# New orders for three engines' lists in a two-layer linear-attention and MLP kernel, and two weight loads issued later

## The chip, the cores and the metric

The kernel runs on one core of a Trainium2 chip. Five engines work side by side in it: TensorE (PE in the profile; its weight loads are PEld), VectorE (DVE), ScalarE (ACT), GpSimd (POOL), and SyncE (SP), which only issues DMAs here. The metric is the device time of one execution in microseconds (us); of several runs the median is given.

## The reference

The input x has 2048 tokens of 512 values. Two layers run one after the other with the same weights. Each is a linear attention and an MLP, both behind a layer norm and both added to x:

```python
phi = lambda t: jnp.where(t > 0, t + 1, jnp.exp(t)) + 1e-6
pq, pk = phi(q), phi(k)                       # 32 heads of 16
kv  = jnp.einsum("bhsd,bhse->bhde", pk, v)
z   = jnp.einsum("bhsd->bhd", pk)
num = jnp.einsum("bhqd,bhde->bhqe", pq, kv)
den = jnp.einsum("bhqd,bhd->bhq", pq, z)[..., None] + 1e-6
x = x + (num / den) @ wo                      # attention, on layernorm(x)
x = x + gelu(layernorm(x) @ w1 + b1) @ w2 + b2    # w1: 512 x 1792
```

## The kernel before, in words

**Tiles.** Tokens lie in 16 tiles of 128 (index st) and 4 chunks of 512 (index c). V is never made: with y the normalised input, the kernel forms G = y'·phi(K) (512 x 512) and from it K'V. The names carry the layer as the code counts it: 0 is layer one, 1 is layer two.

**Names and lines.** Each operation has a name: its kind, the layer, and the tile or chunk and part.

- Norm of a tile: stats (L742), aggr (L744), veps (L755, L747), pow (L757, POOL), nmr (L774), norm (ACT L777 or DVE L782). Its transpose is a DMA issued by SP (TA before the attention, TB before the MLP, L792), or PE products (PT, L805) with a copy tc (L815).
- K and Q: products L860, L878, L891. Each is followed by phi: exp (ACT L830), relu (ACT L841), min (DVE L843), and the sum phi (L847, on DVE or POOL). In the other form it is min (L834) and phi (L836) on DVE, without relu.
- G: L961 in layer one, where it stays in four PSUM banks until the copies cpg0_0 to cpg0_3 (DVE L977). In layer two it is made by chunks (L993), gathered by ga (L1000, L1003) and gt (L1006).
- z: za (L914) sums phi(K) tiles, zhi (L920) and zlo (L923) split the sum in two, ZH (L930) and Z (L942) are products, zsh and zs (L934, L951) and zb (L1022) and dz (L1027) prepare it, ZR (L1030) and cpz (L974) make a row of it.
- K'V: KV (L1016, four short products for each of four row blocks of G), kvm (DVE mask, L1035), M (times wo, L1039), cpm (L974 on ACT, L977 on DVE).
- Denominators: D (L1085), ln (L1087) and rec (L1089) on ACT, pr (L1093) for some chunks. Others go by token: pz (L1061), red (L1064), den (L1067), rec (L1069), pr (L1073), and a transpose TP by SP (L1077).
- WO: L1109, and the sum RA (L1114). MLP: W1 products L1141, gelu (ACT L1147), W2 products L1180, RB (L1186, L1190), the output DMA OD (L1192).
- Late weight loads from POOL's queue (L682): w1_1, wv, wo, w1_0, w2_0, w2_1.

**What sets the order.** Nothing is decided on the chip. `CONF["ORDER"]` holds, for each engine, the list of its operations by name. A planner (`Scheduler.run`) plays the five lists against each other with assumed durations. It gives each tile a PSUM bank or a buffer when its first user is placed, the one that is free first, so that an order also settles which earlier users a tile has to wait for. The buffers that count here: 4 of exp (eb), 4 of relu (rb), 8 of phi(K) (pkb), 2 of ln (lr), 12 of chunks (t4). `assign_waits` turns every dependency on another engine into a semaphore wait, and `play` issues the list:

```python
for o in order[eng]:
    if o.table is not None and o.table != table:
        table = o.table
        e.preload_act_table_set(sets[table])
    for s, v in o.waits:
        e.wait_ge(s.h, v)
    ins = o.fn(e)
```

An engine works its list strictly in order: what waits holds all that stands behind it.

Of the kernel before, what the change touches and what calls it, by code (L numbers as in the profile page):

```python
# [282 lines left out]
def assign_waits(graph, order, sems, dma_sems):  # L283
# [10 lines left out]
    while len(done) < total:  # L294
        moved = False
        for e in ENGINES:
# [117 lines left out]
        "dve":  # L414
# [962 lines left out]
```

## Time and profile before

| what | us |
|---|---|
| median of 3 runs | 326.45 (326.38 to 326.69) |
| the profiled execution | 326.46 |
| its span, first to last instruction | 324.7 |
| outside the span | 1.76 |
| PE busy | 320.7 (1729 matmuls) |
| DVE, ACT, POOL busy | 218.6, 195.2, 134.9 |
| DMA moved | 20.39 MB, 63 GB/s in the mean |

How to read it: "busy" of PE includes the pipeline's own latency, and a row of the timeline runs from the start of its first instruction to the end of its last. So a stall of PE is read from the starts: four 512-column products that follow each other without a wait start 0.216 us apart, the next group 0.864 us behind the first. A number in square brackets is the idle time of the engine ahead of the row, with what ended it.

### The profile page before, as it was taken

What the parts mean: (1) busy time and instruction counts of PE and PEld (TensorE: products, weight loads), DVE (VectorE), ACT (ScalarE), POOL (GpSimd) and SP (SyncE); (2) the same over time, 40 slices, a digit from 0 to 9 for tenths busy, and PEclk for the clock granted to TensorE, in tenths of its full rate; (3) what the DMA queues carried; (4) which work ended last, traced back from release to release, by engine and by line L of the source; (5) the groups of instructions that cost most, each with busy time, mean ns of one, the idle gap of its engine ahead of it and who ended that gap; (6) DMA issues with size and microseconds to landing.
All of it is one profiled execution on the core that took longest, in us unless ns stands there. A gap on an engine that the chain in (4) does not pass through costs nothing.

```text
span 324.7 us, 4792 instructions
## 1 busy us (share of the span) xinstructions
PE 320.7 (99%) x1729; PEld 158.4 (49%) x1729; DVE 218.6 (67%) x506; ACT 195.2 (60%) x336; POOL 134.9 (42%) x224
## 2 busy tenths in 40 slices
PE   8999999999999999999999999999999999999996
PEld 4444544675444444444444444458644444444443
DVE  5997779999985760213759999999999564000232
ACT  6999698773136129488974567869832543576000
POOL 4673276628803259000266735683541754000000
PEclk9999999999999999999999999999999999999999
DMA  7524558112320205310003200022133123000004
GB/s 241 179 43 89 145 166 296 42 38 49 77 52 5 46 16 91 74 32 2 0 0 68 48 16 2 17 50 50 33 67 81 33 51 81 16 0 2 32 27 153
DMA packets 47028, 20.39 MB, mean 63 GB/s; under 512 B 42076, under 2 KB 45532, under 8 KB 47004
## 3 DMA queue, kind: packets, MB, share of 16 engines
q1 hardware_dynamic: 45532, 15.06, 20.2%
q0 software_dynamic: 1056, 4.72, 4.5%
q10 hardware_dynamic: 416, 0.30, 0.3%
q8 instruction: 14, 0.23, 0.3%
q14 instruction: 10, 0.08, 0.1%
HBM read 8.00 MB, written 2.10 MB: 31 GB/s over the span
## 4 chain that ended last, share of the span: by engine, by line
PE 90%; DVE 6%; ACT 2%; DMA 1%; POOL 0%; issue 0%
PE ps L1141 30%; PE ps L1180 28%; PE ps L1109 9%; PE ps L860 7%; PE ps L878 5%; PE ps L993 3%; PE ps L961 3%; PE ps L891 2%; PE ps L1167 1%; DMA t<-in_A_x_dram 1%; DVE eb L843 1%; DVE gtb L977 1%; DVE gacc L1003 1%; DVE yb L782 1%; PE ps L942 1%; PE ps L805 1%
## 5 line engine op out<-in xcount | busy, mean ns | idle before, releaser
L1147 ACT ACTIVATE gT<-ps,b1c 128x512 bf16<-128x512 f32 (+1 forms) x140 | 77.0, 600 | 63.3 <-PE ps L1141 62.6
L1141 PE MATMUL ps<-t,w 128*128 128x512 bf16 (+1 forms) x560 | 101.4, 336 | 0.0
L1180 PE MATMUL ps<-w,gT 128*128 128x512 bf16 x434 | 98.2, 379 | 0.0
L1141 PEld LDWEIGHTS ps<-t,w 128*128 128x128 bf16 x560 | 54.6, 98 | 43.9 <-ACT t L815 0.3
L1180 PEld LDWEIGHTS ps<-w,gT 128*128 128x128 bf16 x434 | 42.5, 98 | 50.0
L757 POOL TENSOR_TENSOR rstd<-veps,neghalf 128x1 f32<-128x1 f32 x64 | 38.7, 616 | 5.3 <-DVE veps L755 3.1
L830 ACT ACTIVATE eb<-ps 128x512 bf16<-128x512 f32 x56 | 32.6, 600 | 12.4 <-PE ps L860 5.5
L1190 DVE TENSOR_TENSOR pkb<-ps,xsb 128x512 bf16<-128x512 f32 x15 | 10.1, 684 | 40.7 <-PE ps L1180 40.7
L742 DVE BATCH_NORM_STATS2 stats<-xsb 128x6 f32<-128x512 f32 x48 | 32.2, 678 | 0.4
L860 PE MATMUL ps<-wqkv,t 128*128 128x512 bf16 x128 | 31.4, 379 | 0.1
L1109 PE MATMUL ps<-gtb,t 128*128 128x512 bf16 x128 | 30.9, 379 | 0.0
L841 ACT ACTIVATE rb<-ps 128x512 bf16<-128x512 f32 x38 | 22.1, 602 | 8.0 <-PE ps L860 6.6
L747 POOL TENSOR_SCALAR veps<-mv 128x1 f32<-128x1 f32 x32 | 8.7, 271 | 43.8 <-DVE mv L744 40.9
L755 POOL TENSOR_SCALAR veps<-mv 128x1 f32<-128x1 f32 x28 | 7.3, 267 | 45.5 <-DVE mv L744 44.0
L777 ACT ACTIVATE yb<-xsb,nmr,rstd 128x512 bf16<-128x512 f32 x21 | 16.9, 809 | 11.7 <-POOL nmr L774 11.7
L782 DVE TENSOR_SCALAR yb<-xsb,mv,rstd 128x512 bf16<-128x512 f32 x27 | 15.7, 590 | 11.9 <-POOL rstd L757 11.7
L1186 DVE TENSOR_TENSOR xsb<-ps,xsb 128x512 f32<-128x512 f32 x16 | 10.9, 682 | 16.5 <-PE ps L1180 16.5
L843 DVE TENSOR_SCALAR eb<-eb 128x512 bf16<-128x512 bf16 x46 | 14.9, 333 | 7.8 <-ACT eb L830 7.6
L878 PE MATMUL ps<-wqkv,t 128*128 128x512 bf16 x80 | 20.1, 379 | 0.0
L860 PEld LDWEIGHTS ps<-wqkv,t 128*128 128x128 bf16 x128 | 12.2, 98 | 15.0 <-ACT t L815 0.5
L1109 PEld LDWEIGHTS ps<-gtb,t 128*128 128x128 bf16 x128 | 12.3, 97 | 14.3 <-ACT gtb L974 0.5
L1126 POOL TENSOR_TENSOR xsb<-xsb,b2b 128x512 f32<-128x512 f32 x14 | 17.3, 1235 | 1.0 <-DVE yb L782 0.7
(103 smaller groups left out, 395.7 us busy)
## 6 DMA issues: line engine op xcount, KB each, us to landing
w<-in_B_w_dram POOLq DMA_DIRECT2D x4, 896.0 KB, 7.2
out_dram<-pkb SPq DMA_DIRECT2D x15, 128.0 KB, 2.0
t<-in_A_x_dram SPq DMA_DIRECT2D x3, 512.0 KB, 6.9
t<-yb SPq DMA_TRANSPOSE x56, 2.5
wqkv<-in_A_wqkv_dram SPq DMA_DIRECT2D x1, 512.0 KB, 5.3
wqkv<-in_A_wqkv_dram POOLq DMA_DIRECT2D x1, 512.0 KB, 4.4
wo<-in_A_wo_dram POOLq DMA_DIRECT2D x1, 512.0 KB, 5.5
t<-t SPq DMA_TRANSPOSE x20, 2.4
```

Source lines behind the costliest of these rows:

```text
L742: G.op("dve", lambda e: e.bn_stats(stats[:, s.slot, :], src()), 602, reads=src_keys, writes=[k + "s"], tiles=[s, *src_tiles], prio=prio, n ...
L757: G.op("pool", lambda e: e.tensor_tensor(rstd[:, s.slot:s.slot + 1], veps[:, s.slot:s.slot + 1], neghalf[:], op=ALU.pow), 530, reads=[k + ...
L782: G.op("dve", lambda e: e.tensor_scalar(yb[:, y.slot, :], src(), stats[:, s.slot, 2:3] if by_act else mv[:, s.slot, 0:1], rstd[:, s.slot:s ...
L830: G.op("act", lambda e: e.activation(eb[:, et.slot, :], bank(bt), ACT.Exp, scale=factor()), 569 if by else 483, reads=[src_key, *more], wr ...
L841: G.op("act", lambda e: e.activation(rb[:, rt.slot, :], bank(bt), ACT.Relu, scale=factor()), 569 if by else 478, reads=[src_key, *more], w ...
L843: G.op("dve", lambda e: e.tensor_scalar(eb[:, et.slot, :], eb[:, et.slot, :], 1.0, 1e-6, op0=ALU.min, op1=ALU.add), 202, reads=[f"e{tag}"] ...
L860: ins = e.matmul(bank(b), lhsT=yTa(yT)[:, dt, k * P:(k + 1) * P], rhs=wqkv[:, dt, D:2 * D], start=(dt == 0), stop=(dt == DT - 1))
L878: ins = e.matmul(bank(b), lhsT=yTa(yT)[:, dt, k * P:(k + 1) * P], rhs=wqkv[:, dt, 0:D], start=(dt == 0), stop=(dt == DT - 1))
L1109: ins = e.matmul(bank(wb), lhsT=yTa(pq)[:, kt, k * P:(k + 1) * P], rhs=gtb[:, kt, :], start=(kt == 0), stop=(kt == DT - 1))
L1141: ins = e.matmul(bank(b, n), lhsT=w1[:, dt, ft * P:(ft + 1) * P], rhs=yTa(yT)[:, dt, k0 * P:k1 * P], start=(dt == 0), stop=(dt == DT - 1))
L1147: G.op("act", lambda e, ft=ft, b=b, k0=k0, k1=k1, n=n: e.activation(gT[:, g.slot, ft * 512 + k0 * P:ft * 512 + k1 * P], bank(b, n), ACT.Ge ...
L1180: ins = e.matmul(bank(b), lhsT=gT[:, g.slot, ft * 512 + k * P:ft * 512 + (k + 1) * P], rhs=w2[:, ft, :], start=(ft == 0), stop=(ft == FT - 1))
```

## The change

The lists of ACT, DVE, POOL and SP are put in another order in two places. PE's list stays the same, and so does every operation, its engine and its form. The diff, cut to the lines that move something:

```diff
         "act":
...
-            "reluq0_1_1 rec0_0_3 cpz0 ln0_0_2 rec0_0_2 ln0_1_0 expq0_2_0 rec0_1_0 ln0_1_1 b1c rec0_1_1 cpm0_1 cpm0_0 "
+            "reluq0_1_1 rec0_0_3 cpz0 ln0_0_2 rec0_0_2 ln0_1_0 expq0_2_0 rec0_1_0 ln0_1_1 rec0_1_1 b1c cpm0_1 cpm0_0 "
...
-            "reluq1_0_0 expq1_0_0 expq1_1_1 expk1_9 reluk1_8 expk1_8 reluk1_9 normA1_12 reluk1_11 expk1_11 expk1_10 "
-            "reluk1_10 reluq1_1_2 expk1_13 expk1_15 reluk1_13 reluk1_15 expq1_1_2 expk1_12 expk1_14 expq1_0_2 "
-            "expq1_0_1 reluq1_0_3 expq1_0_3 reluq1_0_1 reluq1_0_2 expq1_1_3 cpz1 ln1_0_0 rec1_0_0 reluq1_1_3 "
...
+            "reluq1_0_0 expq1_0_0 expq1_1_1 expk1_9 reluk1_8 expk1_8 reluk1_9 normA1_12 reluk1_11 expk1_11 reluq1_1_2 "
+            "expk1_10 expq1_1_2 reluk1_10 reluk1_13 reluk1_15 expk1_13 expk1_15 expk1_12 expq1_0_1 expk1_14 expq1_0_2 "
+            "expq1_0_3 reluq1_0_2 expq1_1_3 reluq1_0_1 reluq1_0_3 cpz1 ln1_0_0 rec1_0_0 reluq1_1_3 reluq1_3_1 ln1_0_1 "
...
         "dve":
...
-            "phiq0_0_1 dz0 minq0_1_0 minq0_1_2 phiq0_1_0 pr0_0_0 minq0_1_1 pr0_0_1 pr0_0_3 cpg0_0 cpg0_1 cpg0_2 "
+            "phiq0_0_1 dz0 minq0_1_0 minq0_1_2 phiq0_1_0 pr0_0_0 pr0_0_1 pr0_0_3 minq0_1_1 cpg0_0 cpg0_1 cpg0_2 "
...
-            "ga1_0_1 mink1_8 minq1_1_1 normA1_13 phik1_9 ga1_1_1 phiq1_1_1 phik1_8 normA1_15 mink1_11 RB0_14 "
-            "statsA1_14 minq1_0_0 aggrA1_14 mink1_10 phik1_11 phik1_10 normA1_14 ga1_1_3 mink1_15 phiq1_0_0 zhi1 "
-            "minq1_1_2 mink1_13 phiq1_1_2 mink1_12 zlo1 ga1_1_2 phik1_13 ga1_1_0 mink1_14 phik1_12 minq1_0_2 phik1_14 "
-            "minq1_0_1 zsh1 ga1_2_1 zs1_3 minq1_0_3 dz1 zb1 minq1_1_3 phiq1_0_2 phiq1_0_3 phiq1_0_1 gt1_1 ga1_2_2 "
...
+            "ga1_0_1 mink1_8 minq1_1_1 normA1_13 phik1_9 ga1_1_1 phiq1_1_1 phik1_8 normA1_15 RB0_14 statsA1_14 "
+            "aggrA1_14 minq1_0_0 mink1_11 phik1_11 minq1_1_2 mink1_10 normA1_14 phik1_10 phiq1_0_0 ga1_1_3 phiq1_1_2 "
+            "ga1_1_0 mink1_15 zhi1 mink1_12 zlo1 ga1_1_2 mink1_13 phik1_13 phik1_12 mink1_14 phik1_14 ga1_2_1 zsh1 "
+            "minq1_0_3 minq1_0_1 zs1_3 minq1_0_2 dz1 zb1 phiq1_0_3 phiq1_0_1 minq1_1_3 phiq1_0_2 gt1_1 ga1_2_2 "
...
-            "RA1_0 rec1_1_2 RA1_1 statsB1_0 rec1_1_3 statsB1_1 aggrB1_1 pr1_1_3 aggrB1_0 RA1_2 statsB1_2 phiq1_3_0 "
-            "aggrB1_2 RA1_5 normB1_0 RA1_3 statsB1_3 aggrB1_3 normB1_2 minq1_3_2 RA1_7 normB1_3 phiq1_3_2 RA1_6 "
...
+            "rec1_1_2 RA1_1 statsB1_0 rec1_1_3 aggrB1_0 statsB1_1 aggrB1_1 RA1_2 pr1_1_3 minq1_3_0 statsB1_2 aggrB1_2 "
+            "normB1_0 phiq1_3_0 RA1_5 RA1_3 statsB1_3 aggrB1_3 normB1_2 minq1_3_2 RA1_7 normB1_3 phiq1_3_2 RA1_6 "
...
         "pool":
...
-            "nmrA0_7 nmrA0_6 vepsA0_11 powA0_11 nmrA0_9 phik0_6 w1_1 phiq0_1_2 wv wo w2_1 w1_0 phiq0_1_1 pr0_0_2 "
-            "pr0_1_0 pr0_1_1 w2_0 pr0_1_2 pr0_1_3 vepsB0_1 powB0_1 vepsB0_0 powB0_0 b20_0 vepsB0_2 powB0_2 vepsB0_3 "
+            "nmrA0_7 nmrA0_6 vepsA0_11 powA0_11 nmrA0_9 phik0_6 w1_1 phiq0_1_2 wv wo w1_0 phiq0_1_1 pr0_0_2 pr0_1_0 "
+            "pr0_1_1 w2_0 w2_1 pr0_1_2 pr0_1_3 vepsB0_1 powB0_1 vepsB0_0 powB0_0 b20_0 vepsB0_2 powB0_2 vepsB0_3 "
...
-            "pr1_0_1 pr1_0_2 pz1_1_3 pr1_0_3 pr1_1_0 phiq1_3_1 pr1_1_2 vepsB1_1 powB1_1 nmrB1_1 vepsB1_0 powB1_0 "
+            "pr1_0_1 pr1_0_2 pz1_1_3 pr1_0_3 phiq1_3_1 pr1_1_0 pr1_1_2 vepsB1_0 vepsB1_1 powB1_1 nmrB1_1 powB1_0 "
...
         "sp":
...
-            "TA1_7 TA1_9 TA1_10 TA1_8 TA1_11 TA1_13 TA1_12 TA1_15 TA1_14 TP1_1_1 TP1_1_0 TP1_1_3 TP1_1_2 TB1_2 TB1_3 "
+            "TA1_7 TA1_9 TA1_10 TA1_8 TA1_11 TA1_13 TA1_12 TA1_15 TA1_14 TP1_1_1 TP1_1_0 TP1_1_2 TP1_1_3 TB1_2 TB1_3 "
```

The cut lines hold the rest of layer two's K'V stage, where the lists are reordered in the same way, and gelu names that only move to another line of the text. Since buffers go to whoever is placed first, some tiles in the two places also take another bank or buffer and so wait for other users; outside the two places the waits are the same, but for the numbers of some t4 buffers.

28 rows, old and new, of the table ORDER are left out of this document.

## The prediction

> **What bounds the kernel.** I read the page's busy times and clock first, then the timeline of PE alone for gaps between starts, then the timelines of DVE and POOL around each gap.
>
> ```profile
> PE 320.7 (99%) x1729; PEld 158.4 (49%) x1729; DVE 218.6 (67%) x506; ACT 195.2 (60%) x336; POOL 134.9 (42%) x224
> ```
>
> PE is busy throughout, and the row PEclk of the page is a 9, the highest digit, in all 40 slices. So time can only be won where PE's starts stand further apart than its pitch: 0.216 us for a 512-column product, so 0.864 for four, and 0.23 for the four short ones of a KV. Past the first 8 us I find two such places (and 0.10 us near 17.5). Layer one's K'V stage:
>
> ```profile
> 48.89 0.38 PE L1085 MATMUL ps<-t,zb 128*128 128x512 bf16 x1
> 49.20 0.40 PE L1016 MATMUL ps<-gtb,wqkv 128*128 128x128 bf16 x4
> 49.44 0.38 PE L1085 MATMUL ps<-t,zb 128*128 128x512 bf16 x1
> 49.80 0.40 PE L1016 MATMUL ps<-gtb,wqkv 128*128 128x128 bf16 x4
> 50.40 0.40 PE L1016 MATMUL ps<-gtb,wqkv 128*128 128x128 bf16 x4 [0.20 <-DVE gtb L977]
> 50.63 1.03 PE L878 MATMUL ps<-wqkv,t 128*128 128x512 bf16 x4
> 51.61 1.04 PE L1039 MATMUL ps<-wo,kvb 128*128 128x512 bf16 x4
> ```
>
> The excess is 49.20-48.89-0.216 = 0.10 ahead of KV0_1, 0.15 ahead of KV0_2, 0.37 ahead of KV0_3, and 51.61-50.63-0.864 = 0.11 ahead of M0_1: **0.73 us**. Layer two, the last phi(K) tiles:
>
> ```profile
> 190.37 1.03 PE L860 MATMUL ps<-wqkv,t 128*128 128x512 bf16 x4
> 191.53 0.18 PE L930 MATMUL ps<-onesm,dz 128*128 128x1 bf16 x1
> ...
> 193.47 1.03 PE L878 MATMUL ps<-wqkv,t 128*128 128x512 bf16 x4
> 194.66 0.55 PE L942 MATMUL ps<-onesm,pkb 128*128 128x1 bf16 x16 [0.17 <-DVE pkb L836]
> ```
>
> 0.30 us ahead of ZH1 (1.16-0.864) and 0.33 ahead of Z1_3: **0.63 us**. Together 1.36: the most that lists can win here, and a floor of 326.46-1.36 = 325.10 us. Why DVE is late, on DVE and then on POOL:
>
> ```profile
> 46.16 1.79 DVE L1093 TENSOR_TENSOR t<-t,lr 128x512 bf16<-128x512 bf16 x1 [0.89 <-ACT lr L1089]
> 47.87 2.47 DVE L977 TENSOR_SCALAR gtb<-ps 128x512 bf16<-128x512 f32 x4
> 50.26 0.89 DVE L834 TENSOR_SCALAR eb<-eb 128x512 bf16<-128x512 bf16 x1
> ...
> 189.83 1.64 DVE L923 TENSOR_TENSOR eb<-zacc,dz 128x512 bf16<-128x512 f32 x1
> ```
> ```profile
> 46.22 1.17 POOL L847 TENSOR_TENSOR t<-eb,rb 128x512 bf16<-128x512 bf16 x1
> ...
> 189.75 1.17 POOL L847 TENSOR_TENSOR pkb<-eb,rb 128x512 bf16<-128x512 bf16 x1 [1.61 <-DVE t L847]
> ```
>
> pr0_0_3 takes 1.79 us where pr0_0_0 and pr0_0_1 took 0.69, and ends 0.56 behind POOL's phiq0_1_1 (47.39). minq0_2_0 takes 0.89 for 0.29 and ends 0.14 behind pr0_1_0 (POOL, 49.84-51.01). zlo1 takes 1.64 and ends 0.55 behind phik1_15 (190.92). A long POOL operation holds DVE operations that work in SBUF, for its whole length. The PSUM copies L977 are not held: the four took 2.47, about 0.6 each, beside POOL work.
>
> The steps below are worked from such rows: the start of the last thing an operation waits for, and durations of its own line. On DVE the next operation may start 0.08 before a row's end: 0.6 apart for 512 columns from PSUM, 0.2 for a min, 0.33 for a bf16 sum; on ACT 0.48 apart; on POOL 1.16 for a long one. A wait on another engine costs 0.04, on POOL 0.08.
>
> **Layer one, step by step** (old clock). minq0_1_1 moves from 43.95, where it lay in DVE's wait for rec0_0_1, to behind pr0_0_3. phiq0_1_1 needs it, so POOL is idle when pr0_0_3 starts at 46.16, and it ends at 46.85. minq0_1_1 runs 46.77-47.05. The copies start at 47.14 instead of 47.87 (now behind G0_11_0, which ends at 47.10) and, 0.6 apart, end at 47.8, 48.5, 49.1 and 49.66. KV0_3 on a stall-free PE is due at 49.77. phiq0_1_1 runs 47.13-48.30 on POOL, before D0_1_1 (48.89); pr0_0_2 follows to 49.54.
>
> Then the tipping point: minq0_2_0 starts at 49.58 and must be ahead of pr0_1_0, which starts at 49.84, set by ACT's rec0_1_0 and unmoved. Margin 0.26. Then KV0_3 ends at 50.16, the masks run from 50.20, kvm0_1 is done at 50.68, M0_1 is due at 50.86: all 0.73 gone. cpm0_1 (old 52.03) shifts with M0_1 to 51.3; ACT has ended rec0_1_1 and b1c, now behind it, by 51.1. So b1c costs nothing; were ACT 0.2 later, WO0_0_0 would use up its slack of 0.2.
>
> On POOL w2_1's issue (0.95) leaves its place ahead of w1_0, which only brings w1_0 forward, and goes behind w2_0: 53.16-54.11. It lies in the wait before pr0_1_2 (1.78 us, old start 54.93, now 54.18). Without that cover 0.95 would reach vepsB0_1, normB0_1, TB0_1 and W1's first product. W2's first product, at 71.5, waits for w2_1 with eleven us to spare.
>
> The transfer is another matter. TB0_1 is issued at 59.02, now 58.29; the median of such a transpose is 2.5, so it landed at 61.46, 0.11 ahead of W10_0_12_0 (61.57, now 60.84). In the view by windows the DMA engines move 346 GB/s at 45-53, 280 at 54.5-57.5 (w2_0), then 0.02 of their time to 60. w2_1 (0.92 MB at 346 GB/s: 2.65 us) now fills 57.2-59.85. The nearest row for a transpose beside a weight load:
>
> ```profile
> t<-yb SPq DMA_TRANSPOSE x56, 2.5
> ...
> b1t<-b1r SPq DMA_TRANSPOSE x1, 7.1
> ```
>
> The tiny Tb1 was issued at 35.38, within w1_1's transfer (35.26, landed 42.32), and took 7.1. If TB0_1 moves only once w2_1 is through, it lands 59.85+1.46 = 61.3 (1.46 as from 60.0, its window's start, to 61.46) and PE stalls 0.47; if they share the engines from 59.3 (a microsecond behind the issue) to 59.85, TB0_1 loses half of that, lands at 61.0, and PE stalls 0.15; if untouched, 0. I take 0.15, since the overlap falls mostly ahead of the transpose's packets: before, hardly any moved in the first microsecond of its 2.44 us. The Trainium skill, "DMA: Bandwidth & Descriptors", section Queues, rings and completion order, says that each DMA engine goes round its queues packet by packet, so that no queue waits for another's whole transfer. By that rule the stall is 0 to 0.15 and the sum at most mine; by Tb1's row it is 0.47 and the sum 0.3 higher. No run here yet shows a transpose of this size beside a load.
>
> **Layer two** (old clock; the first gain shifts all alike). RB0_14 still waits for W20_14_7 (181.90). DVE's new order then runs stats, aggrA1_14 (183.56 instead of 184.46, as minq1_0_0, held by za1_9 to 184.3, now stands behind it), mink1_11, phik1_11 (184.8), minq1_1_2 (185.1: on ACT reluq1_1_2 and expq1_1_2 now stand around expk1_10 and end at 184.74), mink1_10 (185.3). On POOL vepsA1_14 and powA1_14 (0.4 and 0.6) follow za1_9 and end at 185.28, so normA1_14 runs 185.3-185.9, not 1.37 long under za1_10 as before, and phik1_10 ends at 186.2. That holds back za1_10 and za1_11, which need it: POOL 186.3-188.75. Then phiq1_0_0, ga1_1_3, phiq1_1_2 (held by za1_10, to 187.8), ga1_1_0 (behind G1_1_0, to 188.66), mink1_15 (188.95), zhi1 (189.35), mink1_12 (189.55), and zlo1 from **189.48**. phik1_15 can't start before 189.75, since its pkb buffer is freed by G1_1_2 (189.67). So zlo1 is ahead by 0.27, ends at 190.2, and phik1_15 follows to 191.25. ZH1 is due at 191.24: 0.30 won.
>
> After that ga1_1_2 to 190.8, mink1_13 (held to 191.45), phik1_13 (191.8), which frees expk1_14's buffer (ACT 191.85-192.45), phik1_12 (192.4), mink1_14, phik1_14 to 193.4. Z1_3 is due at 194.04: 0.33 won. zb1 is ready at 196.2 for D1_0_0 at 196.4; gt1_3 at 203.65 for KV1_3 at 203.96; kvm1_0 at 204.87 for M1_0 at 205.05.
>
> What comes late next: pr1_1_1, pr1_1_0 and pr1_1_3 do not move forward, as minq1_3_1 and rec's now queue behind pr1_0_3. TP1_1_3 would land at 215.8 with WO1_7_0 due at 215.86 (slack was 0.93), and RA1_5, which frees its bank, ends at 215.66. TP1_1_2, sent first, is safe. A miss costs 0 to 0.3; I take 0.06. Beyond, DVE keeps 0.4 of lag against PE, but the first waits of PE on DVE there have over 0.45 of slack.
>
> **Sum:** 326.46 - 0.73 + 0.15 - 0.63 + 0.06 = **325.3 us**. The profiled execution stands at the median of the runs (326.45), so no correction.
>
> **The rivals.**
>
> - Layer two wins only half: zlo1 starts after 189.75 (against it: 0.27 of margin; for it: seven operations ahead in a row, two held by POOL) and ZH1 still waits 0.30; or TP1_1_3 misses by 0.3. 325.6 us.
> - Layer one wins nothing: minq0_2_0 falls behind pr0_1_0, ends at 51.15 as before, and M0_1 stays at 51.6. For it: the margin hangs on four copies in a row at 0.6. 326.46-0.63+0.06 = 325.9.
> - Neither: both tips miss, or new bank and buffer holders open waits of the same size. 326.4.
> - Slower: TB0_1 behind w2_1's transfer, as Tb1 behind w1_1. At Tb1's 7.1 it lands at 65.4 and W10_0_12_0 waits 4.5: 326.46+4.5-1.36 = 329.6. It ends above the old time once TB0_1 lands after 60.84+1.36 = 62.2. For it: Tb1's row; against it: w2_1 should be through at 59.85, and of 77 transposes Tb1 alone met a load from POOL's queue, from that load's start.
>
> **How the numbers follow.** About 0.2% (0.65 us) is what a measurement of this kernel tells from no change: the line is 325.8. Chances: forecast 0.57 (325.0 to 325.5), half of layer two 0.18, layer one nothing 0.11 (half of it on either side of the line), neither 0.07, slower 0.07. Faster 0.57+0.18+0.05 = 0.80; same 0.13; slower 0.07. The range goes from the floor with the spread of the runs, 325.0, to 326.0, which takes in the second rival and leaves out 0.14.
>
> **What would show it.** Right: L1093's longest row in the stage back at 0.69, KV0_1, KV0_2 and KV0_3 0.44 and 0.23 apart, M0_1 at 50.9, zlo1 at 0.7 and ending before phik1_15, no bracket ahead of L942. Wrong: L834 still 0.89 before the masks; a gap ahead of the first L1141; transposes there of 3 us or more; a gap ahead of the last two L1109 before L1141 in layer two.

## The result and the profile after

| | us | ratio to before |
|---|---|---|
| before, first measurement | 326.40 median of 9 runs (326.07 to 327.04) | |
| changed kernel, first measurement | 327.29 median of 9 runs (327.16 to 327.65) | 1.0027 (1.0018 to 1.0036) |
| changed kernel, measured again on another occasion | 326.90 median of 12 runs (325.91 to 328.86); before 326.60 | 1.0009 (0.9991 to 1.0027) |

So the kernel is 0.9 us slower in the first measurement and 0.3 in the second, whose interval also holds no change; 1.15 faster was forecast. Of the loads only w2_1 is issued later, at 53.63 us instead of 44.52; w1_0 goes out earlier and w2_0 keeps its place. The profiled execution took 327.16 us (span 325.4). From its page:

```profile
PE 320.5 (98%) x1729; PEld 159.7 (49%) x1729; DVE 216.5 (67%) x506; ACT 195.3 (60%) x336; POOL 134.4 (41%) x224
...
L1141 PE MATMUL ps<-t,w 128*128 128x512 bf16 (+1 forms) x560 | 101.4, 336 | 1.5 <-issue 1.5
```

The second row is new: PE now stands idle ahead of W1's products (L1141). First the two places where time was to be won. PE's timeline in layer one's K'V stage (start, length, line, what, count):

```profile
49.12 0.39 PE L1016 MATMUL ps<-gtb,wqkv 128*128 128x128 bf16 x4
49.35 0.38 PE L1085 MATMUL ps<-t,zb 128*128 128x512 bf16 x1
49.56 0.39 PE L1016 MATMUL ps<-gtb,wqkv 128*128 128x128 bf16 x4
49.79 0.38 PE L1085 MATMUL ps<-t,zb 128*128 128x512 bf16 x1
50.00 0.61 PE L1016 MATMUL ps<-gtb,wqkv 128*128 128x128 bf16 x8
50.45 1.03 PE L878 MATMUL ps<-wqkv,t 128*128 128x512 bf16 x4
51.31 1.03 PE L1039 MATMUL ps<-wo,kvb 128*128 128x512 bf16 x4
```

Steps of 0.23, 0.21 and 0.23, KV0_2 and KV0_3 merged into one row of eight, and 0.86 to M0_1: the 0.73 us is gone. Layer two, same view:

```profile
191.71 1.03 PE L860 MATMUL ps<-wqkv,t 128*128 128x512 bf16 x4
192.57 0.17 PE L930 MATMUL ps<-onesm,dz 128*128 128x1 bf16 x1
...
194.50 1.03 PE L878 MATMUL ps<-wqkv,t 128*128 128x512 bf16 x4
195.36 0.54 PE L942 MATMUL ps<-onesm,pkb 128*128 128x1 bf16 x16
```

Both steps are 0.86, and the bracket ahead of L942 is gone: 0.63 us won. Then the place where it was lost, PE's timeline at the first W1 product:

```profile
60.40 1.04 PE L1109 MATMUL ps<-gtb,t 128*128 128x512 bf16 x4
62.93 3.33 PE L1141 MATMUL ps<-t,w 128*128 128x256 bf16 x29 [1.50 <-issue]
```

and in the kernel before:

```profile
60.70 1.04 PE L1109 MATMUL ps<-gtb,t 128*128 128x512 bf16 x4
61.57 2.70 PE L1141 MATMUL ps<-t,w 128*128 128x256 bf16 x23
```

62.93 - 60.40 - 0.864 = **1.66 us**, where it was nothing before; it is the only stall over 0.1 us past the first 9 us. It waits for TB0_1, the transpose issued at 58.72: it landed at 62.84, after 4.12 us where it took 2.44 before. The two gains and this loss make +0.30. Another 0.46 lies at the start, so that the two together come a little above the two profiles' difference (0.70): G0_15_0 began at 18.12 instead of 17.67, ahead of anything that the change moves. In the twelve profiles of this study it began at 17.54 to 18.27 (where its own record is missing, I put it 0.216 ahead of the next product), in no order that follows the edits, so I take it for chance. That does not explain why all nine runs of the first measurement lie within 327.16 to 327.65, some 0.6 above what +0.30 gives; this stays open.

What did TB0_1 wait for? The DMA queues of the changed kernel in two stretches, 60 to 61 and 61 to 62.3 us (packets, MB, the packets' times added up as a share of the 16 engines' time; q0 carries the loads issued by POOL, q1 the transposes, q8 the instruction fetches):

```profile
q1 hardware_dynamic: 499, 0.12, 194.9%
q0 software_dynamic: 34, 0.07, 22.6%
q8 instruction: 1, 0.02, 7.0%
```
```profile
q1 hardware_dynamic: 45, 0.01, 6.1%
```

and of the kernel before at 60 to 61:

```profile
q1 hardware_dynamic: 539, 0.13, 64.7%
```

Before, TB0_1's 544 packets were through within the microsecond, and alone. Now two things are in the way. The end of w2_1's stream (q0) runs to 60.3. And a 16 KB instruction fetch runs as one packet from 60.25 to 61.36, which before had run at 57.73, right behind w2_0's stream. 45 of TB0_1's packets, about one engine's share (544/16 = 34) and a few, moved only once the fetch was over; the last at 62.2. That the fetch and these packets share one engine is inferred from their number, as the view does not name engines.

That gives two theories. **A**: the fetch on one DMA engine holds the last packets. **B**: the load itself holds the transpose. They part where one of the two is missing.

### The profile page after: what moved, and what is told of

It is laid out like the page before. It is cut to its first block, busy times and chain, and to the rows that moved or that the text cites. A ratio compares the mean times of both kernels' runs of the same rounds, so it can differ in the third digit from the quotient of the medians.

```text
span 325.4 us, 4795 instructions
## 1 busy us (share of the span) xinstructions
PE 320.5 (98%) x1729; PEld 159.7 (49%) x1729; DVE 216.5 (67%) x506; ACT 195.3 (60%) x336; POOL 134.4 (41%) x224
## 4 chain that ended last, share of the span: by engine, by line
PE 98%; issue 0%; DVE 0%
PE ps L1141 30%; PE ps L1180 29%; PE ps L860 9%; PE ps L1109 8%; PE ps L878 5%; PE ps L961 4%; PE ps L993 4%; PE ps L891 3%; PE ps L698 1%; PE ps L1167 1%; PE ps L1085 1%; PE ps L805 1%; PE ps L942 1%; PE ps L1016 1%; PE ps L1039 1%
## 5 line engine op out<-in xcount | busy, mean ns | idle before, releaser
L1141 PE MATMUL ps<-t,w 128*128 128x512 bf16 (+1 forms) x560 | 101.4, 336 | 1.5 <-issue 1.5
L1141 PEld LDWEIGHTS ps<-t,w 128*128 128x128 bf16 x560 | 54.7, 98 | 45.4 <-issue 2.0
L1109 PE MATMUL ps<-gtb,t 128*128 128x512 bf16 x128 | 30.9, 379 | 0.0
L782 DVE TENSOR_SCALAR yb<-xsb,mv,rstd 128x512 bf16<-128x512 f32 x27 | 14.1, 533 | 11.5 <-POOL rstd L757 11.2
L1109 PEld LDWEIGHTS ps<-gtb,t 128*128 128x128 bf16 x128 | 12.4, 97 | 14.3 <-ACT gtb L974 0.5
```

The lines of the kernel that those rows point to most:

```text
L1109: ins = e.matmul(bank(wb), lhsT=yTa(pq)[:, kt, k * P:(k + 1) * P], rhs=gtb[:, kt, :], start=(kt == 0), stop=(kt == DT - 1))
L1141: ins = e.matmul(bank(b, n), lhsT=w1[:, dt, ft * P:(ft + 1) * P], rhs=yTa(yT)[:, dt, k0 * P:k1 * P], start=(dt == 0), stop=(dt == DT - 1))
```

## The experiments

**1. w2_1 put back (changed kernel, POOL's list).**

```diff
- ... wv wo w1_0 phiq0_1_1 ... pr0_1_1 w2_0 w2_1 pr0_1_2 ...
+ ... wv wo w2_1 w1_0 phiq0_1_1 ... pr0_1_1 w2_0 pr0_1_2 ...
```

> The changed kernel with w2_1's issue put back ahead of w1_0 in POOL's list; all other new lists stay. Both theories (A: TB0_1 is late because a 16 KB instruction fetch, itself put back by w2_1's stream, sits ahead of its packets; B: TB0_1 is late because w2_1's transfer is in flight) expect no wait ahead of W10_0_12_0, TB0_1 back at 2.4 to 2.5 us, and the fetch of that stretch back at about 57 us. If the layer-one and layer-two gains (0.73 and 0.63) are real and the 0.46 by which the changed kernel's profile started later is chance: 326.40 - 1.36 = 325.0. If the 0.46 belongs to the new lists: 325.5. If I am wrong on the gains: about 326.4.

Measured: 325.40 (325.12 to 325.66), before 326.71 beside it: 0.9962 (0.9950 to 0.9974), 1.31 us won of the 1.36 in the sum. PE's timeline of this run:

```profile
59.99 1.04 PE L1109 MATMUL ps<-gtb,t 128*128 128x512 bf16 x3
60.87 3.36 PE L1141 MATMUL ps<-t,w 128*128 128x256 bf16 x29
```

No wait; TB0_1 took 2.44. The fetch ran at 53.87, not at about 57. So the gains are real, and the 0.46 at the start is not the lists' doing.

**2. w2_1's move alone (kernel before).**

```diff
- ... wv wo w2_1 w1_0 phiq0_1_1 ... w2_0 pr0_1_2 ...
+ ... wv wo w1_0 phiq0_1_1 ... w2_0 w2_1 pr0_1_2 ...
```

> The kernel before with nothing changed but w2_1's issue, which moves behind w2_0. Both theories expect the whole loss and none of the gains: TB0_1 lands about 4 us after its issue instead of 2.44, and W10_0_12_0 waits 1.5 to 1.7 us: 326.40 + 1.6 = 328.0. A expects a 16 KB fetch to start when w2_1's stream ends (about 60.5 us) and TB0_1's last packets to move only when it is over. Rival to both (the wait comes from the new lists of DVE or POOL and not from the load): 326.4, no wait.

Measured: 327.91 (327.41 to 328.13), 1.0035 (1.0022 to 1.0048). TB0_1 took 4.26, the fetch ran at 60.32, and W10_0_12_0 waited 1.80:

```profile
63.00 1.25 PE L1141 MATMUL ps<-t,w 128*128 128x256 bf16 x10 [1.64 <-issue]
```

But "none of the gains" was wrong. DVE's long row in the K'V stage shows it:

```profile
46.47 1.23 DVE L1093 TENSOR_TENSOR t<-t,lr 128x512 bf16<-128x512 bf16 x1 [0.89 <-ACT lr L1089]
```

pr0_0_3 took 1.23 instead of 1.79. With w2_1's issue out of the way, phiq0_1_1 starts half a microsecond sooner on POOL against pr0_0_3 (at 46.00, 0.47 ahead of it; before at 46.22, 0.06 behind it) and lets go of DVE sooner; of the 0.73, only 0.08 is left. 1.80 - 0.65 = +1.15; measured +1.20.

**3. The fetch moved, the load left (changed kernel).**

```diff
-    N_WARM2=4 ... N_WARM=8
+    N_WARM2=36 ... N_WARM=0
```

> The changed kernel; the 12 dummy products at PE's start (8 of 512 columns and 4 of 128) become 36 of 128 columns: the same 4608 columns, 24 more products, so each instruction fetch of PE comes 24 products earlier. w2_1's load stays where the change put it. The fetch that ran at 60.25 after 356 products (in the kernel before at 57.73 after 342) should then fall between 51 and 53 us, in the pause between w1_0's and w2_0's streams. A expects TB0_1 to land about 1 us after w2_1's stream ends, at 61.0 to 61.4, W10_0_12_0 to wait 0.2 at most, and 327.3 - 1.5 = 325.8, or 325.3 if the start is 0.46 earlier too. B expects TB0_1 still at 62.8, the wait of 1.66 still there, 327.3. Both leave out that the other fetches move too.

Measured: 326.46 (325.63 to 327.64), 0.9998 (0.9987 to 1.0010). The fetch ran at 53.48, in the pause. TB0_1 took 3.05, its last packets at 61.3, and

```profile
61.96 2.23 PE L1141 MATMUL ps<-t,w 128*128 128x256 bf16 x19 [0.43 <-issue]
```

61.96 less the due time of 61.37 (the last L1109 product, at 61.15, and one pitch) is a wait of 0.59. So both theories hold in part: without the fetch the load alone costs 0.6, and the other microsecond is the fetch. The total fell less than hoped, because the later fetches moved too and hit others: TA1_8 took 4.40 with a fetch at 174.06, and PE waited 0.70 for it (and 0.28 near 223):

```profile
177.19 1.04 PE L860 MATMUL ps<-wqkv,t 128*128 128x512 bf16 x4 [0.54 <-DMA t<-yb]
```

**4. w2_1 later still (changed kernel).**

```diff
- ... w2_0 w2_1 pr0_1_2 ... vepsB0_3 powB0_3 phiq0_2_3 ...
+ ... w2_0 pr0_1_2 ... vepsB0_3 powB0_3 w2_1 phiq0_2_3 ...
```

> The changed kernel with w2_1's issue put later still, behind powB0_3, in a wait of POOL of 3.5 us; its stream then runs at about 62.5 to 65.5 us, beside TB0_2 and TB0_3 in place of TB0_1, and the fetch of that stretch should be back at about 57.5 us, ahead of all of them. Both expect TB0_1 on time and no wait ahead of W10_0_12_0: 325.0 to 325.6. A expects the transposes beside the load, with no fetch near them, to take 3.0 us or less; B expects TB0_2 or TB0_3 to take 4 us or more.

Measured: 330.34 (328.76 to 331.35), 1.0115 (1.0094 to 1.0136), the worst of all, and against both totals. The stream ran later than I had put it, at 65.5 to 69.4. TB0_1 was on time and the fetch at 57.62, but TB0_3 took 6.13 and TP0_2_0 4.14, with no fetch near them. B's half, alone and in full size. The queues in 67.5 to 68.5, the middle of w2_1's stream:

```profile
q0 software_dynamic: 91, 0.37, 95.0%
q1 hardware_dynamic: 90, 0.02, 10.2%
```

In this microsecond one packet of the transpose goes for each packet of the load, 90 to 91. But a packet of the load carries 4 KB and one of the transpose 256 B: of 544 packets, 90 move in a microsecond that would hold them all. Earlier it was less: at 65.5 to 67.0 the load moved 46 packets and the transpose, issued at 64.28, none. So the transpose is in effect behind the stream, and landed 1.1 us after the stream's last full packets (69.3). The loss has a second part. PE's timeline, and then PE's busy time, clock, DMA share and GB/s by stretches:

```profile
65.80 1.47 PE L1141 MATMUL ps<-t,w 128*128 128x256 bf16 x12
70.50 4.08 PE L1141 MATMUL ps<-t,w 128*128 128x256 bf16 x24 [3.23 <-issue]
```
```profile
67.00:70.00 3.00, 0.27 (x3) 0.96 1.11 321
70.00:71.00 1.00, 0.50 (x3) 0.50 0.20 28
71.00:72.00 1.00, 1.00 (x7) 0.50 0.00 0
72.00:73.00 1.00, 1.00 (x6) 0.50 0.00 0
73.00:74.00 1.00, 1.00 (x11) 0.90 0.00 0
```

PE waits 3.40 for the first product that reads TB0_3's columns, and comes back at half clock for 2.7 us (70.5 to 73.2), which costs 1.30 more. -1.36 + 3.40 + 1.30 = +3.3; measured +3.6.

**5. The changed kernel again.** No edit.

> The changed kernel once more, with nothing altered, for one question: in its profile the first G product came 0.46 us later than in the profile of before, ahead of everything that the change touches. If that start is chance, as the five starts seen since suggest (G0_15_0 at 17.67 to 18.42 in six profiles), then by the traces the change is worth -1.36 + 1.66 = +0.3 us, 0.1%, and this measurement should lie nearer to that than the first (+0.89); if it belongs to the change, +0.8 again. In the profile: TB0_1 4.1 to 4.3 us, W10_0_12_0 1.6 to 1.9 us late, a fetch that starts at the end of w2_1's stream.

Measured: 326.90 (325.91 to 328.86), +0.30. Its profile, of the fastest of the twelve runs (325.91), is the comparison that I could not have built: the same program, but here the fetch went at 54.02, 0.03 us ahead of w2_0's first packet. TB0_1 took 3.17. PE's timeline, and the queues at 60 to 61:

```profile
60.09 1.04 PE L1109 MATMUL ps<-gtb,t 128*128 128x512 bf16 x3
61.67 2.56 PE L1141 MATMUL ps<-t,w 128*128 128x256 bf16 x22 [0.54 <-issue]
```
```profile
q1 hardware_dynamic: 532, 0.13, 92.9%
q0 software_dynamic: 20, 0.03, 9.2%
```

No q8, and the wait is 0.71 where it was 1.66 with the fetch. My expectation of 1.6 to 1.9 missed; the two profiles of one kernel split the loss into 0.71 for the load and 0.95 for the fetch. The start, 17.84, was again its own.

**6 and 7. Each place's lists alone (kernel before).** Layer one's two edits, and then layer two's lists without them:

```diff
-ln0_1_1 b1c rec0_1_1 ... / pr0_0_0 minq0_1_1 pr0_0_1 pr0_0_3 ...
+ln0_1_1 rec0_1_1 b1c ... / pr0_0_0 pr0_0_1 pr0_0_3 minq0_1_1 ...
```

> The kernel before with layer one's two list edits alone (minq0_1_1 behind pr0_0_3, b1c behind rec0_1_1); w2_1 stays ahead of w1_0, layer two is untouched. If the lists alone open the stage: no wait from KV0_0 to M0_1, 0.73 won, nothing lost at TB0_1, 0.63 still lost in layer two: 0.7 us under before. Rival: these lists win only with w2_1's issue out of phiq0_1_1's way: 0.1 us under before. (w2_1's move alone has taken 0.65 of the 0.73.)

> The kernel before with layer two's list edits alone. If the two places add up: no wait ahead of ZH1 and Z1_3, the 0.73 of layer one still there: 0.63 us under before. With the layer-one lists alone it should add up to the -1.31 of the run with w2_1 put back. Rival: layer two's lists win only when layer one shifts them: 0.3 or less.

Measured: layer one's lists 325.79 (324.93 to 326.87), 0.9976 (0.9963 to 0.9989), -0.81; layer two's 325.96 (325.74 to 326.36), 0.9973 (0.9958 to 0.9988), -0.64. Each place's stalls are gone in its own run and there in the other's, and the sum, -1.45, agrees with the -1.31 and -1.44 of the runs with w2_1 put back. The profile taken of layer one's run was its slowest execution (326.87): there w1_0 and w2_0 landed 1.6 and 1.9 late, the fetch fell at 59.26, TB0_1 took 3.69 and W10_0_12_0 waited 1.23. Ahead of TB0_1 even w2_0's load has little room.

**8 and 9. The fetch a little earlier and a little later (changed kernel).**

```diff
-    N_WARM2=4 ... N_WARM=8           # 8
+    N_WARM2=12 ... N_WARM=6
-    held = idle(..., [P] * cf["N_IDLE"][k], ...)    # 9
+    held = idle(..., [[D] * 2, [P]][k], ...)
```

> The changed kernel with 6 more of the dummy products at PE's start (6 of 512 columns and 12 of 128 in place of 8 and 4; the same 4608 columns), which brings each instruction fetch about 6 products, 1.3 us, forward. Theory now: the load alone holds TB0_1 back by 0.6 to 0.7 us, and the fetch adds 1.0 when it is asked for (after some 326 products, about 54 us) later than the first packets of w2_0's stream (54.0), because it then moves only behind w2_1's stream, ahead of TB0_1's last packets. Here it is asked for at about 53, always in time: fetch at 52.5 to 53.5, TB0_1 3.0 to 3.2 us, a wait of 0.6 to 0.7 ahead of W10_0_12_0, and before - 1.36 + 0.65 = 0.7 us under before. Rival (the fetch is not what splits the two profiles of the changed kernel): TB0_1 4.1 us, the median 0.3 to 0.9 above before.

> The changed kernel with 6 products fewer at the start (idle0_0's 8 dummies of 128 columns become 2 of 512), so that the fetch is asked for at about 55.4, always within w2_0's stream. Theory: it moves only when w2_1's stream ends (60.2 to 60.4), TB0_1 takes 4.1 to 4.3 us, W10_0_12_0 waits 1.6 to 1.8, and the median is before - 1.36 + 1.7 = 0.3 above before, and 1.0 above the run with the earlier fetch. Rival: no difference between the two.

Measured: 327.06 (326.24 to 327.73), 1.0012 (1.0003 to 1.0021), and 327.24 (326.57 to 327.59), 1.0014 (1.0005 to 1.0023). Run 8 failed as an experiment: the fetch didn't come forward. It ran at 59.69, in run 9 at 60.17, both at the end of w2_1's stream; the fetches from the fifth on moved by -7 to +7 products in run 8, where repeats of one kernel differ by 4 at most. So what sets the moment of a fetch is more than a count of products, and stays open. By the times both rivals came out, but since the fetch did not come forward, these two runs do not test them. What both show is the loss with the fetch in place: TB0_1 4.32 and 4.52, waits of 1.86 and 2.05, so +0.50 and +0.69 by the sum, +0.41 and +0.59 measured.

**10. Run 1 again, beside 8 and 9.**

> Once more the changed kernel with w2_1 put back ahead of w1_0, beside the two above on one chip. No wait of PE past 8 us, 1.3 us under before, 0.6 under the run with the earlier fetch and 1.6 under that with the later one.

Measured: 325.21 (325.01 to 325.63), before 326.65: 0.9955 (0.9943 to 0.9968). No wait of PE past 8 us; the fetch ran at 57.30 here. This version, the new lists with w2_1 where it was, beats both kernels.

## Why the prediction was wrong, point by point

- **Layer one's lists, -0.73: right.** minq0_2_0 began at 50.05 and pr0_1_0 at 50.30, the 0.25 of margin that was worked out (0.26). pr0_0_3 took 0.69:

```profile
46.62 0.69 DVE L1093 TENSOR_TENSOR t<-t,lr 128x512 bf16<-128x512 bf16 x1 [0.89 <-ACT lr L1089]
...
50.05 0.29 DVE L834 TENSOR_SCALAR eb<-eb 128x512 bf16<-128x512 bf16 x1
```

- **Layer two's lists, -0.63: right.** zlo1 and phik1_15 after:

```profile
190.82 0.68 DVE L923 TENSOR_TENSOR eb<-zacc,dz 128x512 bf16<-128x512 f32 x1
```
```profile
191.09 1.43 POOL L847 TENSOR_TENSOR pkb<-eb,rb 128x512 bf16<-128x512 bf16 x1 [0.87 <-PE ps L993]
```

  zlo1 starts 0.27 ahead and takes 0.68 instead of 1.64, as put.
- **TP1_1_3 and WO1_7_0, +0.06: nothing.** The transpose landed at 216.90 and RA1_5 ended at 216.82, for a product due at 217.17.
- **w2_1's issue "only brings w1_0 forward": wrong.** Run 2 shows that the move alone takes 0.65 of layer one's 0.73. It didn't count, since the lists take all of it without the move (run 6): the two edits win the same time, and only one of them costs something.
- **TB0_1 beside w2_1's transfer, +0.15 with bounds 0 to 0.47: this is the step that failed.** It measured 1.66, 0.71 and, in other kernels with the same move, 1.80, 1.86 and 2.05. The stream's end was well placed (59.85 put; 60.3 measured, in a profile that began 0.46 later), and the mechanism of the upper bound, TB0_1 moving once w2_1 is through, was the right one; without a fetch that term is 0.59 to 0.71, above even the bound of 0.47. I took a third of it, on the ground that the two would share the engines evenly and that the transpose would lose half of the overlap. They share by packets at best, 90 to 91 in run 4, and the transpose's are 1/16 of the size. So the rule that I cited from the Trainium skill ("DMA: Bandwidth & Descriptors", section Queues, rings and completion order) agrees with that microsecond, and what I concluded from it does not hold: a queue waits for no whole transfer, but here the transpose's small packets hardly moved beside the load's large ones.
- **The rest, 0.95 to 1.3, was in no term at all.** The instruction fetch is in the page of before (q8, 14 packets, 0.23 MB), and its price could be read there: TA1_0, TB1_6 and TB1_14 took 4.08, 3.95 and 4.03 instead of 2.4 to 2.5, each with a 16 KB fetch and no load in its window, all three off PE's path. Tb1, my nearest row, had the fetch of 39.08 in its 7.1 us as well. The fetch at 57.73 stood right at the end of w2_0's stream; that it might follow the end of a longer one, and so land on TB0_1, could be suspected. It could not be known: the fetch at 39.08 ran amid w1_1's stream.
- **The slower rival** had the right place and sign ("TB0_1 behind w2_1's transfer"; the kernel loses once TB0_1 lands after 62.2, and it landed at 62.84, or 62.4 without the later start). It had the wrong size and a chance of 0.07, because I let the sharing argument speak against it.
- **No correction for the start** was right for before (its profile stands at the median), but a single profile's start is uncertain by 0.7 us, nearly as much as the whole effect.

## What to carry to other kernels

Price a transfer that is moved at the place where it lands, for what else is in the DMA engines then: here a transpose's small packets beside a weight load's large ones were as good as behind it. Look up the instruction fetches too; with a longer stream, one came later and fell on a transpose that it used to miss. And when a change removes a stall in two ways at once, try each way alone, as one may be all gain and the other all price.

## What the runs showed of the hardware

- A 16 KB instruction fetch is one packet and lasts 0.9 to 1.7 us; a transpose in whose window it starts, 1.2 to 2.2 us behind the issue, lands after 3.94 to 4.52 us instead of 2.4 to 2.5. The Trainium skill, "Runtime: NRT & Kernel Launch", section Instruction fetch mechanics, has the 16 KB blocks of 256 instructions and calls the cost of crossing one "mostly hidden"; for the instructions themselves no run here speaks against that, but for a transpose on PE's path it was a microsecond.
- The fetch of this stretch ran at a stream's end or ahead of it, in no profile amid one: 57.73 (before), 60.25, 60.32, 59.69 and 60.17, each at the end of the last load's stream, and 54.02 where it was 0.03 us ahead of one. That it is asked for at about 54 us and then waits for a stream that is already moving is inferred from these. It is no rule: in the kernel before the fetch at 39.08 ran while w1_1's stream took 89% of the 16 engines' time (39.0 to 39.5). What sets the two apart is open.
- Load and fetch don't add up in the transpose's own time: 2.44 without either, 3.05 and 3.17 with the load, 3.94 to 4.40 with the fetch (other transposes, the fetch 1.2 to 2.2 us behind their issue), 4.12 to 4.52 with both.
- A wait of 3.40 us cost PE its clock (granted 0.50 from 69.8 to 73.2, 1.30 us lost); waits of 1.66 to 2.05 did not. The Trainium skill, "TensorE: Matmul & The Clock Gate", Part 1, gives an idle window of about 3.4 us for that. Here the clock fell sooner, 2.5 us after PE's last product had ended (67.27), which is why the row of 67 to 70 has 0.96.
